# Attention with beacon keys, then two expert layers: the first sequence's queries are cut at 512, its masks become matmuls, and its last 64 queries follow between expert groups

## The chip, the cores and the metric

The kernel runs on one core of one Trainium2 chip. Its time is the device time in microseconds (us) of one execution; three runs of the kernel before gave 326.47, 326.90 and 327.72 us, with a median of 326.9 us. The core has five engines that matter here: TensorE (PE) for matmuls and transposes, ScalarE (ACT) for exponentials and activations, VectorE (DVE) for copies and sums, GpSimd (POOL) for masks and for the issue of most DMAs, and SyncE (SP) for the issue of the others. PE writes only to PSUM, a memory of few banks, from which ACT and DVE fetch the results.

## What is computed

```python
k_all = np.concatenate([beacon_k, k], axis=2)      # 8 x 8 heads, 16 + 576 keys of 64
v_all = np.concatenate([beacon_v, v], axis=2)
scores = scale * np.matmul(q, k_all.transpose(0, 1, 3, 2))
causal[:, Nb:] = np.triu(np.ones((S, S), dtype=bool), k=1)
scores = np.where(causal, -1000000000.0, scores)
a = np.exp(scores - scores.max(-1, keepdims=True))
a /= a.sum(-1, keepdims=True) + 1e-09
x = np.matmul(a, v_all)                            # then reshaped to 4608 tokens x 512
h = x @ w_in                                       # 512 x 2048
out = np.maximum(0.01 * h, h) @ w_out              # 2048 x 512
```

There are 8 sequences of 576 tokens with 8 heads of 64. Inputs and output are float32; the kernel works in bfloat16 on chip.

## The kernel before

**Pairs and steps.** Two heads make a pair (128 partitions), so there are 32 pairs, `g` = 0 to 31, four to a sequence. A pair goes through these steps, each with a letter in strings such as `"q4 v2.1 x1"` that `run` (L698) carries out one after the other. The order of the strings is the order on every engine: `tc.manual_schedule` takes it as it stands.

- `l` loads q or k of a pair (POOL issues the DMA), `V` loads a block of values, `i` and `o` load a half of the up and down weights (1 MB each in bfloat16).
- `q`, `k` (`t_q`, L231) transpose q or k in 18 small matmuls by the identity and copy the result from PSUM.
- `s` (`score`, L256) multiplies keys by queries. Keys stand on partitions in five blocks of up to 128 (`NKB`, `ROWS`, the first with the 16 beacon keys); a block is multiplied only by the queries that may see it. The four steps s0 to s3 of a pair have 512, 464, 416 and 288 columns for each head (`SCORES`, L50), the two heads in the two halves of the array. ACT takes the exponential of each step in one instruction (L276). Two score buffers of PSUM alternate (`ps_sc`, `bufs=2`).
- `m` (`mask`, L282) sets what lies under the diagonal to zero, five selections on POOL for a pair (L289).
- `v` (`value`, L374) multiplies the exponentials by the values, in two halves of 128-query tiles: t = 0, 1, 2 and t = 3, 4. A 65th column of ones gives the sum by which DVE then divides (L388, L389). `e` and `W`, `value_ahead` and `unused_ahead`, stand for beginning a half early and for fillers in its bank.
- `x` (`x_transposes`, L400) turns the result and copies it to `xT`, the experts' input.
- `w` (`unused`, L653) are fillers: matmuls of a blank tile whose result nobody reads; `w2.384` is two of 384 columns.
- `u` (`up`, L629) is one step of the first expert layer: for a chunk of 512 tokens, 128 of the 2048 hidden columns, four matmuls of 512 columns (L442) and one activation on ACT (L450). `d` (`down`) is one step of the second layer; for chunk 0 it is a quarter of the hidden dimension for 128 tokens, four matmuls (L512).

Chunk 0 is tokens 0 to 511 of sequence 0, so its first `u` needs all four pairs of that sequence.

**Opening and main loop.** The strings at L751 to L770 write out sequences 0 and 1 by hand (pairs 0 to 7) with all 16 up steps of chunk 0 and the first six down steps. The first up step comes after the `x` of pair 3, and the scores of pair 4 already stand ahead of it. Then a loop over pairs 8 to 31 sorts events by planned times and calls `fill` (L602) between them, which interleaves up and down steps. There the q and k come by DMA transposes and the scores in stretches of 512 columns (L314).

**Queues.** POOL issues the DMAs of q, k, v and weights in program order between its masks, each one waiting for the eighth before it to land. SP issues the first keys, the DMA transposes and the stores. `gT` (L429) holds an expert chunk's activations, two buffers of 16 x 512 columns for the chunks in turn.

Of the kernel before, what the change touches and what calls it, by code (L numbers as in the profile page):

```python
# [15 lines left out]
def kernel(  # L16
# [40 lines left out]
    PADS = (1392, 1728)  # L57
    BASE = [0, 512, 976, 1440, 1648]
    QT = [(0, 112), (112, 128), (240, 128), (368, 128), (496, 80)]
    NA, NK = 4, 8  # L60
# [7 lines left out]
    def acol(g, c, q0):  # L68
        if g >= LAID:
            return FLAT[c] + q0 - OFF[c]  # L70
        if c == 0:
            return 1312 if q0 == 496 else q0
        if c == 4:
            return 1648
        return BASE[c] + q0 - OFF[c]
# [13 lines left out]
    blank = singles.tile([128, 128], BF16, name="blank")  # L89
    w_in_sb = [singles.tile([128, NJ, DF // 2], BF16, name=f"w_in_sb{i}") for i in range(2)]  # L90
# [26 lines left out]
    def make_pads():  # L117
        nc.vector.memset(k_all[:, :, NB + S :], 0.0)
        for t in a_bufs:
            for c in PADS:  # L120
                nc.vector.memset(t[:, :, c : c + 48], 0.0)

    def make_ones():
        for t in v_bufs:
            nc.vector.memset(t[:, :, :, D : D + 1], 1.0)
# [3 lines left out]
    def load_w_in(i):  # L129
        n = DF // 2  # L130
        loaded["w_in", i] = nc.gpsimd.dma_start(
            out=w_in_sb[i], in_=w_in_r[:, :, i * n : (i + 1) * n]
        )
# [71 lines left out]
    def load_v_cast(b, c):  # L205
        dst = v_bufs[b % 2]
        lo = 0
        if c == 0:
            nc.gpsimd.dma_start(
                out=dst[0:NB, 0, :, 0:D], in_=beacon_v[b].rearrange("h p d -> p h d")  # L210
            )
            lo = NB
        n = ROWS[c] - lo
        nc.gpsimd.dma_start(  # L214
            out=dst[lo : ROWS[c], c, :, 0:D],
            in_=v[b, :, OFF[c] : OFF[c] + n].rearrange("h p d -> p h d"),
        )
# [13 lines left out]
    def t_q(g, which, copy):  # L231
        b, hp, grp, rows = where(g)
        dst = operand(g, which)
        ps = ps_one.tile([128, 1024], BF16, name="tp", tag="one")
        psv = ps[:, 0:S].rearrange("c (i p) -> c i p", i=RI)
        for i in range(RI):
            if (g, which) == (0, 1):
                nc.tensor.transpose(
                    psv[:, i], k_nat0[:, i].rearrange("p h d -> p (h d)"), ident[0:RP, 0:RP]
                )  # L240
                continue
            for par in range(2):
                nc.tensor.transpose(
                    psv[par * 64 : par * 64 + 64, i], qk_raw[b, grp][which][rows, par, i], ident[rows, rows]
                )
        cut = 13 if (g, which) == (0, 1) else RP
        for lo, hi, eng in ((0, cut, copy), (cut, RP, nc.vector.tensor_copy)):
            if lo < hi:
                eng(
                    out=dst.rearrange("c (p i) -> c p i", i=RI)[:, lo:hi],  # L250
                    in_=psv.rearrange("c i p -> c p i")[:, lo:hi],
                )

    probs = {}

    def score(g, n):  # L256
# [4 lines left out]
        parts = SCORES[n]  # L261
        sc = ps_sc.tile([128, 2, 512], FP32, name="sc", tag="sc")
        c0 = parts[0][3]
        for c, q0, w, col in parts:
            for par in range(2):
                ps_ = slice(par * 64, par * 64 + 64)
                nc.tensor.matmul(  # L267
                    out=sc[:, par, col - c0 : col - c0 + w],
                    lhsT=kT[ps_, c * 128 : (c + 1) * 128],
                    rhs=qT[ps_, q0 : q0 + w],  # L270
                    start=True,
                    stop=True,
                    skip_group_check=True,
                )
        w = sum(p[2] for p in parts)
        nc.scalar.activation(  # L276
            out=aT[:, :, c0 : c0 + w], in_=sc[:, :, 0:w], func=AF.Exp, scale=0.125
        )
# [66 lines left out]
    xs, avs = {}, {}  # L345

    begun = set()

    def value_matmuls(g, half, avv, ts):
# [3 lines left out]
        for t in ts:  # L353
            q0, _ = QT[t]
            for par in range(2):
                n = t % 3 * 2 + par
                for c in range(t + 1):
                    a0 = acol(g, c, q0)
                    nc.tensor.matmul(  # L359
                        out=avv[:, n, 0 : D + 1],  # L360
                        lhsT=aT[0 : ROWS[c], par, a0 : a0 + 128],
                        rhs=va[0 : ROWS[c], c, 2 * hp + par, :],
# [5 lines left out]
    def value_ahead(g):  # L368
        if (g, 0) not in avs:
            avs[g, 0] = ps_one.tile([128, 512], FP32, name="av", tag="one")  # L370
        value_matmuls(g, 0, avs[g, 0][:, 0:396].rearrange("p (n w) -> p n w", w=66), (0, 1))
        begun.add(g)

    def value(g, half):  # L374
        if half == 0:
            xs[g] = (
                headpool.tile([128, 5, 2, D], BF16, name="x_nat", bufs=4),
                headpool.tile([128, 10], FP32, name="rec"),
            )
        x_nat, rec = xs[g]  # L380
        t0, t1 = ((0, 3), (3, 5))[half]
        av = avs.pop((g, half), None)
        if av is None:
            av = ps_one.tile([128, 512], FP32, name="av", tag="one")
        avv = av[:, 0 : (t1 - t0) * 132].rearrange("p (n w) -> p n w", w=66)
        value_matmuls(g, half, avv, range(t0 + (2 if half == 0 and g in begun else 0), t1))
# [6 lines left out]
            op=ALU.mult,  # L393
        )
# [5 lines left out]
    def x_transposes(g, copy):  # L400
        b, hp = divmod(g, NPAIR)
        x_nat, _ = xs.pop(g)
        ps = ps_one.tile([128, 1024], BF16, name="tp", tag="one")
        for t, (q0, rows) in enumerate(QT):
            nc.tensor.transpose(
# [4 lines left out]
        copy(out=xT[:, hp, x_at(b) : x_at(b) + S], in_=ps[:, 0:S])  # L410
# [17 lines left out]

    gT = {}  # L429
# [235 lines left out]
    def unused_ahead(g, half, n):  # L665
        if (g, half) not in avs:
            avs[g, half] = ps_one.tile([128, 512], FP32, name="av", tag="one")
        for i in range(n):
            nc.tensor.matmul(
                out=avs[g, half][:, 400:512], lhsT=blank, rhs=blank[:, 0:112], start=True, stop=True  # L670
            )

# [19 lines left out]
    def run(steps):  # L692
        for step in steps.split():
# [7 lines left out]
            elif op == "e":  # L701
                value_ahead(*a)
# [22 lines left out]
            elif op == "W":  # L725
                unused_ahead(*a)
            elif op == "i":
                load_w_in(a[0])
# [17 lines left out]
    with order:  # L746
# [5 lines left out]
        make_identity(nc, ident, nomemset=True)  # L752
        make_ones()
        run("l1.1 l2.0 l2.1 V0.0 V0.1 l3.0 l3.1 V0.2 V0.3 V0.4 l4.0 l4.1 i0")
# [7 lines left out]
        run("q0.1 k0 w2.384 s0.0 m0.0 w3.256 s0.1 q1 s0.2 m0.1 k1 s0.3 m0.2")  # L762
        run("w2.384 s1.0 m1.0 q2 s1.1 k2 w2.384 s1.2 m1.1 w2.384 s1.3 m1.2 W0.0.4 s2.0 m2.0 W0.0.4 s2.1 W0.0.6 q3 l5.0 l5.1 s2.2 k3 w4.384 v0.0 m2.1 s2.3 i1 m2.2 W0.1.4 s3.0 m3.0 v1.0 s3.1 v0.1 s3.2 v1.1 m3.1 l6.0 l6.1 s3.3 x0.1 m3.2")
        run("v2.0 V1.0 V1.1 q4 v2.1 x1 k4.1 v3.0 v3.1 x2.1 s4.0 s4.1 x3 m4.0 V1.2 V1.3 V1.4 l7.0 l7.1 u u s4.2 s4.3 q5 k5 m4.1 m4.2 u o0 u")
        load_beacon_k(2, B, nc.gpsimd)
        run("s5.0 s5.1 m5.0 u u u s5.2 s5.3 q6 k6 m5.1 m5.2 o1 u u s6.0 s6.1 m6.0 u v4.0 u v4.1 y4 N8.0 N8.1 u s6.2 s6.3 q7 k7 m6.1 m6.2 u")
        cast_beacon_k(2, B, nc.gpsimd.tensor_copy)
        run("u v5.0 u v5.1 N9.0 s7.0 s7.1 m7.0 d x5 v6.0 v6.1 T8 d s7.2 s7.3")
        beacon_transposes(2, B)
        run("m7.1 m7.2 N9.1 u b8.2 b9.2 b10.2 b11.2 x6 v7.0 T9 v7.1 d d d N10.0 N10.1 d V2.0 V2.1 x7 t0 T10")  # L770
# [97 lines left out]
```

## Time and profile before

| what | value |
|---|---|
| median of three timed runs | 326.9 us |
| the profiled execution's own time | 325.23 us |
| its span in the profile | 323.5 us |
| PE busy, 3429 matmuls | 317.3 us (98%) |
| ACT busy | 199.3 us (62%) |
| POOL busy | 184.7 us (57%) |
| DVE busy | 146.1 us (45%) |
| first score matmul starts | 7.04 us |
| first up matmul starts | 25.25 us |
| granted PE clock | full throughout |

The profile is of one execution; times in it count from the start of the span, and the 1.7 us between the span and the execution's own time lie outside it. A row of a timeline gives start, length from the first start to the last end, engine, line, operation, what is written and read, the rows and columns of the array, the number of columns, and how many instructions follow one another. Matmuls overlap: a single one is in flight for about 0.2 us or more while the next starts, so the distance from one row's start to the next row's start says what a row takes, not its length. A waits row gives who waited for whom, the sum in us and how often.

### The profile page before, as it was taken

How to read it: one execution, taken by the hardware profiler on the slowest of the kernel's cores; microseconds unless marked ns; L12 is line 12 of the kernel's file. 1: busy time of each engine (PE TensorE's matmuls, PEld its weight loads, DVE VectorE, ACT ScalarE, POOL GpSimd, SP SyncE). 2: the span in 40 equal slices, each digit the busy share in tenths (PEclk: the TensorE clock that was granted, in tenths of full speed). 3: DMA queues.
4: the chain of work that ended last, by engine and by line, in shares of the span. 5: the costliest groups of instructions: out<-in, count | busy, mean ns of one | idle time of the engine just before them, and what ended most of it. 6: DMA issues, size and time to landing. Idle time of an engine off the chain costs nothing.

```text
span 323.5 us, 8521 instructions
## 1 busy us (share of the span) xinstructions
PE 317.3 (98%) x3429; PEld 213.4 (66%) x3429; DVE 146.1 (45%) x297; ACT 199.3 (62%) x336; POOL 184.7 (57%) x354
## 2 busy tenths in 40 slices
PE   8999999999999999999999999999999999999995
PEld 5574565445687558845888888656865785466684
DVE  3473354518446145434552455345444542325444
ACT  4969862487765786478647873786468415653420
POOL 8895968999997687659875977664221000000000
PEclk9999999999999999999999999999999999999999
DMA  8999999999999999999999999999112112000203
GB/s 140 137 206 175 147 214 120 188 165 190 157 138 169 218 147 107 124 174 80 154 192 160 110 127 115 196 128 135 52 53 79 24 54 97 2 1 32 79 20 132
DMA packets 155928, 39.93 MB, mean 123 GB/s; under 512 B 143040, under 2 KB 153152, under 8 KB 155888
## 3 DMA queue, kind: packets, MB, share of 16 engines
q0 software_dynamic: 99824, 18.54, 91.3%
q1 hardware_dynamic: 55792, 20.77, 37.1%
q8 instruction: 27, 0.44, 0.6%
q14 instruction: 13, 0.11, 0.1%
q10 hardware_dynamic: 272, 0.07, 0.1%
HBM read 37.22 MB, written 9.44 MB: 144 GB/s over the span
## 4 chain that ended last, share of the span: by engine, by line
PE 77%; DMA 10%; POOL 5%; ACT 3%; DVE 2%; issue 2%; DVEq 0%; POOLq 0%; ACTq 0%
PE acc L442 31%; PE acc L537 30%; PE av L359 6%; PE sc L314 6%; DMA w_out_sb<-in_moe_w_out_dram 4%; PE acc L512 4%; DMA w_in_sb<-in_moe_w_in_dram 4%; POOL aT L289 2%; DMA gsum<-in_k_dram 2%; ACT aT L333 2%; POOL gsum L158 2%; ACT aT L329 1%; DVE p L565 0%; ACT gT L450 0%; DVE u L565 0%
## 5 line engine op out<-in xcount | busy, mean ns | idle before, releaser
L442 PE MATMUL acc<-xT,w_in_sb 128*128 128x512 bf16 (+1 forms) x640 | 135.7, 358 | 0.3 <-ACT aT L329 0.3
L450 ACT ACTIVATE gT<-acc 128x512 bf16<-128x512 f32 x144 | 82.8, 621 | 46.4 <-PE acc L442 46.2
L442 PEld LDWEIGHTS <-w_in_sb 128*128 128x128 bf16 x640 | 59.6, 98 | 52.4 <-issue 2.9
L289 POOL TENSOR_SCALAR_AFFINE_SELECT aT<-aT 128x256 bf16<-128x256 bf16 (+2 forms) x160 | 59.7, 404 | 51.7 <-ACT aT L329 30.9
L537 PEld LDWEIGHTS <-gT 128*128 128x128 bf16 x512 | 48.8, 98 | 9.1 <-issue 1.8
L333 ACT ACTIVATE aT<-sc 128x1024 bf16<-128x1024 f32 (+3 forms) x64 | 51.8, 895 | 0.0
L537 PE MATMUL acc<-w_out_sb,gT 128*128 128x256 bf16 x384 | 46.2, 273 | 0.4 <-ACT gT L450 0.4
L329 ACT ACTIVATE aT<-sc 128x512 bf16<-128x512 f32 (+3 forms) x64 | 29.0, 522 | 27.9 <-PE sc L314 27.7
L388 DVE RECIPROCAL rec<-av 128x6 f32<-128x6 f32 (+1 forms) x64 | 12.0, 188 | 67.0 <-PE av L359 66.3
L359 PEld LDWEIGHTS <-aT 128*128 128x128 bf16 (+1 forms) x960 | 36.7, 98 | 8.3 <-issue 0.6
L537 PEld LDWEIGHTS <-gsum 128*128 128x128 bf16 x384 | 36.5, 98 | 6.2 <-issue 0.4
L359 PE MATMUL av<-v_aug,aT 128*128 128x65 bf16 (+1 forms) x960 | 39.4, 194 | 0.3 <-ACT gT L450 0.2
L214 POOL DMA_DIRECT2D v_aug<-in_v_dram x40 | 34.2, 859 | 4.1 <-DMA w_in_sb<-in_moe_w_in_dram 3.4
L568 ACT COPY p<-acc 128x512 f32<-128x512 f32 (+1 forms) x25 | 14.5, 580 | 35.6 <-PE acc L537 35.6
L171 POOL DMA_DIRECT2D k_nat<-in_k_dram x48 | 34.9, 733 | 1.3 <-DMA w_out_sb<-in_moe_w_out_dram 0.6
L171 POOL DMA_DIRECT2D q_nat<-in_q_dram x48 | 34.8, 731 | 0.6 <-issue 0.3
L389 DVE TENSOR_TENSOR x_nat<-av,rec 128x384 bf16<-128x384 f32 (+1 forms) x64 | 31.4, 491 | 2.2
L537 PE MATMUL acc<-w_sum,gsum 128*128 128x256 bf16 x256 | 31.9, 273 | 0.0
L276 ACT ACTIVATE aT<-sc 128x1024 bf16<-128x1024 f32 (+3 forms) x32 | 25.9, 875 | 3.5 <-PE sc L267 3.5
L620 DVE TENSOR_TENSOR gsum<-gT 128x1024 bf16<-128x1024 bf16 x16 | 11.0, 688 | 28.1 <-ACT gT L450 28.1
L314 PE MATMUL sc<-qT,kT 64*128 64x80 bf16 (+22 forms) x384 | 22.0, 250 | 0.3
L314 PEld LDWEIGHTS <-kT 64*128 64x128 bf16 x384 | 12.9, 94 | 10.9 <-issue 7.6
(62 smaller groups left out, 227.3 us busy)
## 6 DMA issues: line engine op xcount, KB each, us to landing
out_dram<-p SPq DMA_DIRECT2D x26, 256.0 KB, 3.2
q_nat<-in_q_dram POOLq DMA_DIRECT2D x48, 72.0 KB, 5.5
k_nat<-in_k_dram POOLq DMA_DIRECT2D x48, 72.0 KB, 5.0
v_aug<-in_v_dram POOLq DMA_DIRECT2D x24, 128.0 KB, 6.1
w_in_sb<-in_moe_w_in_dram POOLq DMA_DIRECT2D x2, 1024.0 KB, 11.7
w_out_sb<-in_moe_w_out_dram POOLq DMA_DIRECT2D x2, 1024.0 KB, 11.7
out_dram<-u SPq DMA_DIRECT2D x8, 256.0 KB, 2.7
gsum<-in_q_dram POOLq DMA_DIRECT2D x8, 144.0 KB, 6.9
```

The costliest lines, as they stand in the source:

```text
L171: nc.gpsimd.dma_start(out=t[:, :, par], in_=(q, k)[which][b, 2 * hp + par].rearrange("(t p) d -> p t d", p=NR),)
L214: nc.gpsimd.dma_start(out=dst[lo : ROWS[c], c, :, 0:D], in_=v[b, :, OFF[c] : OFF[c] + n].rearrange("h p d -> p h d"),)
L276: nc.scalar.activation(out=aT[:, :, c0 : c0 + w], in_=sc[:, :, 0:w], func=AF.Exp, scale=0.125)
L289: nc.gpsimd.affine_select(out=view, in_=view, compare_op=ALU.is_ge, fill=0.0, base=128 - n if lo == 0 else 0, channel_multiplier=-1, patte ...
L314: nc.tensor.matmul(out=(sc[par] if apart else sc[:, par])[:, at : at + b - a], lhsT=kT[ps_, c * 128 : (c + 1) * 128], rhs=qT[ps_, q0 : q0 ...
L329: nc.scalar.activation(out=probs[g][:, par, lo:hi], in_=sc[par][:, at : at + hi - lo], func=AF.Exp, scale=0.125)
L333: nc.scalar.activation(out=probs[g][:, :, lo:hi], in_=sc[:, :, at : at + hi - lo], func=AF.Exp, scale=0.125)
L359: nc.tensor.matmul(out=avv[:, n, 0 : D + 1], lhsT=aT[0 : ROWS[c], par, a0 : a0 + 128], rhs=va[0 : ROWS[c], c, 2 * hp + par, :], start=(c = ...
L389: nc.vector.tensor_tensor(out=x_nat[:, t0:t1].rearrange("p t e d -> p (t e) d"), in0=avv[:, :, 0:D], in1=rec[:, n0:n1, None].to_broadcast( ...
L442: nc.tensor.matmul(out=acc[:, lo:hi], lhsT=w_in_cols(fc, j), rhs=xT[:, j, x0 : x0 + hi - lo], start=(j == 0), stop=(j == NJ - 1), skip_gro ...
L450: nc.scalar.activation(out=gT[i][:, fc, :], in_=acc, func=AF.Prelu, alpha=0.01)
L537: nc.tensor.matmul(out=acc[:, lo : lo + HD], lhsT=left(i, n, fc, tile), rhs=right(n, fc), start=(lo == 0 and fc == 0), stop=(fc == HF - 1) ...
```

## The change

Sequence 0 only (`g < NPAIR`):

- Its scores cover queries 0 to 511 (`CUT`), in three steps of 512, 400 and 432 columns (`EARLY`) for four. The masks of these blocks are added to the scores in PSUM by matmuls of the identity by a `bias` tile (`hide`), ten for a pair, and the POOL masks of sequence 0 go. The bias is made on POOL between the identity and the next DMA issue.
- The value halves become t = 0, 1 and t = 2, 3, 4; the last tile and key block have 16 rows.
- The other 64 queries are copied aside by DVE when q is transposed (`rest_q`, in the still unused `gT` of chunk 1). Their scores, in 64 columns for each key block, follow as steps `L0` to `L3` between up steps of chunk 0 (`rest_scores`); their values for two pairs each as `Y0` and `Y1`, and their transposes as `Z0` and `Z1`, after the sixteenth up step.
- Steps `q4`, `k4`, `s4.0` and `s4.1` stand after the first up steps, no longer ahead of them; values and `x` of pairs 4 to 7 come after all up steps of chunk 0. Eleven down steps for six stand ahead of the main loop.
- Loads: q and k of pair 3 ahead of all values; the last block of values in two parts; the first half of the up weights in two parts, ahead of pairs 4 and 5; the second half ahead of pairs 6 and 7.
- Fillers from the first scores to the first up: 27 of 384 columns, where there were 10 of 384, 3 of 256 and 18 of 112.

```diff
-    PADS = (1392, 1728)
+    PADS = ((1344, 112), (1728, 48))
+    CUT = 512
+    REST = S - CUT
+    EARLY = [[(0, 0, 512, 0)], [(1, 112, 400, 512)], [(2, 240, 272, 912), (3, 368, 144, 1184), (4, 496, 16, 1328)]]
...
+    def make_bias():
+        nc.gpsimd.affine_select(
+            out=bias, in_=blank, compare_op=ALU.is_ge, fill=-32768.0,
+            base=0, channel_multiplier=-1, pattern=[[1, 128]],
+        )
...
+        if which == 0 and g < NPAIR:
+            nc.vector.tensor_copy(out=rest_q[:, g], in_=dst[:, CUT:S])
...
+        if g < NPAIR:
+            for c, q0, w, col in parts:
+                w, at = min(w, 112 if c == 0 else 128), 16 if c == 0 else 0
+                for par in range(2):
+                    hide(sc[:, par, col - c0 : col - c0 + w], at)
...
+    def hide(out, at):
+        nc.tensor.matmul(out=out, lhsT=ident, rhs=bias[:, at : at + out.shape[1]], start=False, stop=True)
+
+    def rest_scores(g):
+        kT = qk[g][1]
+        sc = ps_sc.tile([128, 2, 512], FP32, name="sc", tag="sc")
+        for c in range(NKB):
+            for par in range(2):
+                ps_ = slice(par * 64, par * 64 + 64)
+                nc.tensor.matmul(
+                    out=sc[:, par, c * REST : (c + 1) * REST],
+                    lhsT=kT[ps_, c * 128 : (c + 1) * 128],
+                    rhs=rest_q[ps_, g],
...
+        for par in range(2):
+            hide(sc[:, par, 4 * REST : 5 * REST], CUT - OFF[4])
+        nc.scalar.activation(out=rest_a[:, g], in_=sc[:, :, 0 : NKB * REST], func=AF.Exp, scale=0.125)
...
+                    rows = min(ROWS[c], CUT - OFF[c]) if g < NPAIR else ROWS[c]
...
+    def rest_values(p):
...
+        for e in range(2):
+            for par in range(2):
+                for c in range(NKB):
+                    nc.tensor.matmul(
+                        out=avv[:, 2 * e + par, 0 : D + 1],
+                        lhsT=rest_a[0 : ROWS[c], 2 * p + e, par, c * REST : (c + 1) * REST],
+                        rhs=v_bufs[0][0 : ROWS[c], c, 2 * (2 * p + e) + par, :],
...
+            rows = min(rows, end - q0)
...
-        run("l1.1 l2.0 l2.1 V0.0 V0.1 l3.0 l3.1 V0.2 V0.3 V0.4 l4.0 l4.1 i0")
+        run("l1.1 l2.0 l2.1 l3.0 l3.1 V0.0 V0.1 V0.2 V0.3 V0.4.0.16 i0.0.2 i0.1.2 l4.0 l4.1 l5.0 l5.1 V0.4.16 i1 l6.0 l6.1 V1.0 V1.1")
...
-        run("q0.1 k0 w2.384 s0.0 m0.0 w3.256 s0.1 q1 s0.2 m0.1 k1 s0.3 m0.2")
-        run("w2.384 s1.0 m1.0 q2 s1.1 k2 w2.384 s1.2 m1.1 w2.384 s1.3 m1.2 W0.0.4 s2.0 m2.0 W0.0.4 s2.1 W0.0.6 q3 l5.0 l5.1 s2.2 k3 w4.384 v0.0 m2.1 s2.3 i1 m2.2 W0.1.4 s3.0 m3.0 v1.0 s3.1 v0.1 s3.2 v1.1 m3.1 l6.0 l6.1 s3.3 x0.1 m3.2")
-        run("v2.0 V1.0 V1.1 q4 v2.1 x1 k4.1 v3.0 v3.1 x2.1 s4.0 s4.1 x3 m4.0 V1.2 V1.3 V1.4 l7.0 l7.1 u u s4.2 s4.3 q5 k5 m4.1 m4.2 u o0 u")
+        run("q0.1 k0 w2.384 s0.0 w1.384 s0.1 q1 s0.2 w2.384 k1 w2.384 s1.0 q2 w1.384 s1.1 w1.384 k2 s1.2 w1.384 q3 w1.384 s2.0 k3 s2.1 w3.384 s2.2 w2.384 s3.0 v0.0 w1.384 s3.1 v1.0 w1.384 s3.2 v2.0 w2.384 v3.0 w7.384")
+        run("v0.1 v1.1 v2.1 x0.1 v3.1 x1.1 w1.384 x2.1 w1.384 x3.1 u u L0 q4 u k4.1 u s4.0 s4.1 m4.0 V1.2 V1.3 V1.4 u L1 u s4.2 s4.3 m4.1 m4.2 l7.0 l7.1 o0 q5 k5 u u")
         load_beacon_k(2, B, nc.gpsimd)
-        run("s5.0 s5.1 m5.0 u u u s5.2 s5.3 q6 k6 m5.1 m5.2 o1 u u s6.0 s6.1 m6.0 u v4.0 u v4.1 y4 N8.0 N8.1 u s6.2 s6.3 q7 k7 m6.1 m6.2 u")
+        run("s5.0 s5.1 m5.0 u u L2 u s5.2 s5.3 m5.1 m5.2 o1 q6 k6 u u s6.0 s6.1 m6.0 u L3 u s6.2 s6.3 m6.1 m6.2 u Y0 N8.0 N8.1 q7 k7 Z0 Y1")
         cast_beacon_k(2, B, nc.gpsimd.tensor_copy)
-        run("u v5.0 u v5.1 N9.0 s7.0 s7.1 m7.0 d x5 v6.0 v6.1 T8 d s7.2 s7.3")
+        run("v4.0 s7.0 s7.1 m7.0 v4.1 y4 Z1 v5.0 s7.2 s7.3 v5.1 N9.0 d v6.0 x5 d v6.1 T8 d")
         beacon_transposes(2, B)
-        run("m7.1 m7.2 N9.1 u b8.2 b9.2 b10.2 b11.2 x6 v7.0 T9 v7.1 d d d N10.0 N10.1 d V2.0 V2.1 x7 t0 T10")
+        run("m7.1 m7.2 N9.1 d b8.2 b9.2 b10.2 b11.2 x6 v7.0 T9 v7.1 d d d N10.0 N10.1 d V2.0 V2.1 x7 t0 T10 d d d")
```

## The prediction

> **What bounds the kernel now.** I read the page's busy shares and chain of waits first, then the busy times by stretch, then TensorE's (PE's) timeline.
>
> ```profile
> PE 317.3 (98%) x3429; PEld 213.4 (66%) x3429; DVE 146.1 (45%) x297; ACT 199.3 (62%) x336; POOL 184.7 (57%) x354
> PE 77%; DMA 10%; POOL 5%; ACT 3%; DVE 2%; issue 2%; DVEq 0%; POOLq 0%; ACTq 0%
> 7.04:25.25 18.21, 17.98 (x369) 11.93 (x368) 11.15 (x25) 14.64 (x20) 17.06 (x37) 1.00 1.75 174
> 25.25:52.24 26.99, 26.60 (x371) 14.59 (x369) 11.16 (x27) 21.19 (x32) 19.21 (x37) 1.00 2.04 168
> ```
>
> PE is the chain. The last two lines are my two stages (columns: length, then busy PE, PE loads, DVE, ACT, POOL): from the first scores (7.04) to the first up matmul (25.25), and from there to the third quarter of the first down tile (52.24). PE is busy in both, but busy is not peak, so I price PE by the distance between starts in its timeline:
>
> ```profile
> 15.33 0.47 PE L243 MATMUL tp<-ident,gsum 64*64 64x64 bf16 x18
> 15.73 0.82 PE L657 MATMUL av<-blank 128*128 128x384 bf16 x4
> 16.39 0.53 PE L359 MATMUL av<-v_aug,aT 128*128 128x65 bf16 x12
> ...
> 27.54 0.76 PE L243 MATMUL tp<-ident,gsum 64*64 64x64 bf16 x36
> 28.23 1.90 PE L442 MATMUL acc<-xT,w_in_sb 128*128 128x512 bf16 x8
> 30.06 0.59 PE L267 MATMUL sc<-qT,kT 64*128 64x512 bf16 x4
> ...
> 37.97 1.03 PE L442 MATMUL acc<-xT,w_in_sb 128*128 128x512 bf16 x4
> 38.83 0.72 PE L359 MATMUL av<-v_aug,aT 128*128 128x65 bf16 x18
> 39.39 1.03 PE L442 MATMUL acc<-xT,w_in_sb 128*128 128x512 bf16 x4
> 40.35 0.48 PE L267 MATMUL sc<-qT,kT 64*128 64x336 bf16 x8
> ```
>
> Four 384-column fillers take 16.39-15.73 = 0.66, so 0.16 us each (2.4 columns per ns). 18 value matmuls take 0.56 (about 30 ns each), 36 transposes 0.69 (19 ns). Four up matmuls take 0.86 ahead of value matmuls (37.97 to 38.83) but 0.96 ahead of scores (39.39 to 40.35): a change of the array's shape (128*128 to 64*128) costs 0.10. Eight ahead of scores take 1.83 = 8 x 0.216 + 0.10. I take 0.097 per change.
>
> Does this price list close? By the instruction order, the first stage of before has 13.1 us of columns (score pairs, which run side by side in two halves, 3.2; q and k transposes 2.7; values 3.5; x transposes 1.0; fillers 2.8) and 41 changes of shape x 0.097 = 4.0: 17.1 against 18.2 elapsed, so 1.1 of real waits. The second stage: 24.4 + 18 x 0.097 = 26.15 against 26.65 up to 51.9. So PE's own work sets both stages. ACT, with 14.64 of 18.21 and 21.19 of 26.99, is not the bound.
>
> **What the Trainium skill says.** "TensorEngine Tiling (Array Packing)", Tiling Modes (Key Properties): "Changing tiling mode (not just tile) drains the TensorE". The trace agrees: 0.10 us per change above. Same page, Performance Considerations (Instruction Overhead): about 60 cycles per matmul however narrow; here 65 columns take 29 to 31 ns, which I use as floor. "TensorE: Matmul & The Clock Gate", Part 3 (The mechanism): matmuls keep strict order, so a filler is paid in full whether needed or not; the trace shows all of them in program order.
>
> **The change, part by part.**
>
> *First stage (s0 to the first up).* Scores of a pair shrink from 1680 to 1344 columns: 4 x 336 / 2.4 = -0.56. Transposes and scores of pair 4 (q4, k4, s4.0, s4.1) move behind the first up: -0.69 - 0.41. Values and x transposes stay in number (120 and 20). The 40 mask matmuls are new: per pair 2 x (112+3x128+16) columns, in all 1.7, with the floor for the narrow ones 1.9. Fillers go from 10 of 384, 3 of 256 and 18 of 112 columns (2.76) to 27 of 384: 4.32, +1.56. Changes of shape go from 41 to 56, +1.45: a score group is now followed by 128-row masks, and the twelve 16-row products and transposes (L424 and L503 of the changed kernel, from cutting at query 512) are built as 32*128 tiles, two changes each, partly shared. Sum: 20.35 against 17.1, +3.2. Waits I leave nearly alone (-0.2): twenty POOL masks vanish (0.5 us of PE load waits on them in the whole opening), but the copy of q0's last 64 columns stands on DVE ahead of the first key copy (unseen; between 0.1 and 0.35, I take 0.28 with its wait on ACT), and everything is behind it. First up: about 25.25 + 3.0 = 28.3.
>
> *What could hide that?* ACT's exponentials of this stage fall from 16 (spaced 0.92, 0.82, 0.74, 0.64) to 12, about 9.7 us for 12.6. ACT had not been the limit, so this buys nothing while PE has 20 us to do. DMA neither: the POOL queue delivers in order; values of sequence 0 were down at 18.8, and the first half-megabyte of up weights, now right behind them, should be down near 21 (half of the 4.3 us that the full half took to arrive), long before 28. The mask constant on POOL (0.32, as the identity) delays the second keys' issue by as much; they are wanted at 10 us. The extra DMA from each split costs POOL 0.7 to 0.8 us of issue, hidden as the first up comes late.
>
> *Second stage and after.* The late scores L0..L3: 40 narrow matmuls in pairs 0.5, 8 masks 0.25. Late values Y0, Y1: 40 x 29 ns = 1.15; transposes 0.1. q4, k4, s4.0, s4.1 arrive: +1.1. Changes of shape: +22 = 2.1 (u to L, L to its masks, u to q4, Y in 64 columns). Sum +5.2 (the model of all matmuls gives 5.1). None of it lies under another engine's work: PE is full to the end, so what is added is paid.
>
> *Waits there.* A late score takes one of the two score buffers between s4.1 and s4.2, so s4.3 waits until ACT has done s4.0, s4.1, an up's activation, L1's exponential: by ACT's spacing 0.92+0.82+0.5+0.7 against PE's u, L1, u, s4.2 of about 2.5. From 0.2 to 0.75 per pair, three times: 1.0 (0.4 to 2.2). In return some waits of before go (columns: us in all, times, longest):
>
> ```profile
> PE acc L512 <- DMA w_out_sb<-in_moe_w_out_dram: 0.3, 1, 0.3
> PE acc L442 <- ACT aT L329: 0.3, 1, 0.3
> ```
>
> The second down weights landed at 52.2 and PE now comes for them later; first stretch of scores the same (its keys landed at 59.6). With what surrounds them 0.5 to 1.4; I take 1.0. More downs ahead of the main loop (11 for 6) only change order. SP's queue keeps its order, with later starts.
>
> *Sum*: 3.2 + 5.1 - 0.2 + 1.0 - 1.0 = +8.1; I use +8. The profiled execution took 325.23 (span 323.5 and 1.7 around it), which gives 333.2; it lies 1.7 below the median of 326.9, which gives 334.9.
>
> **Rivals.**
>
> *Small tiles come cheap.* No row of before shows a 32*128 tile. If changing to it drains nothing, 24 changes fall away: -2.3, so +5.6, 332.5. Lower bound, with masks also streaming behind the scores at no change: +4. Against: 64*128, 64*64 and 128*64 all cost 0.10.
>
> *Buffers bite.* The score-buffer waits come out at 0.75 each (+1.2), and the first stage's own waits (s1.0 on k1's copy 0.45, values at the 37 ns they had before 20 us instead of 30: 0.7) add 1.2: +10.5, 337.4.
>
> *ACT sets the first up* (not slower). In before the first up follows the last exponential's end by 25.25-21.09 = 4.2:
>
> ```profile
> 17.20 3.89 ACT L276 ACTIVATE aT<-sc 128x576 bf16<-128x576 f32 x5 [0.84 <-PE sc L267]
> 24.98 0.43 PE L405 MATMUL tp<-ident,x_nat 112*128 112x112 bf16 x5
> 25.25 1.95 PE L442 MATMUL acc<-xT,w_in_sb 128*128 128x512 bf16 x8
> ```
>
> If the exponentials were the limit and PE only filled time, they would end near 7.9+9.7 = 17.6 and the first up come at 21.8: -3.5. With +5.1 behind it and up to 1.6 of waits gone, 0.0: 326.9, and faster if the first up comes before about 21.7. For: the stage is full of fillers. Against: even without fillers PE has 16 us from 7.3.
>
> That the change does not do what it says is ruled out by the order: all its steps stand where it puts them.
>
> **How the numbers follow.** Main case 0.55, small tiles cheap 0.22, buffers bite 0.10, ACT sets it 0.13. The last splits at no change: faster by over 0.5% 0.07, within 0.5% 0.06, the others all slower: 0.87. Half a per cent (1.6 us) is about what a measurement of this kernel can tell from no change. The range reaches from inside the cheap-tile case, with its waits gone, 329.5, to just past buffers bite, 337.5; it leaves out the last rival and a little above.
>
> **What would show it.** First up at 28.3 (27 to 29) for 25.25; mask matmuls 47 to 55 ns apart and 0.10 lost at each switch, also around the 16-row ones; PE gaps at s4.3, s5.3, s6.3 with ACT's late exponential as releaser; no wait for down weights; the stretch from first up to third down 4 us longer. A first up before 25 would make me wrong, as would a second stage no longer than before.

## The result, and the profile after

The changed kernel took 337.8 us (median of six) against 326.4 for the kernel before (median of six in the same rounds): a ratio of 1.034, with a 95% interval of 1.031 to 1.038. It is slower, as forecast, by 11 us where 8 were forecast, and lies 0.3 us above the top of the range. In some executions, the first profiled one of the changed kernel among them, PE's clock ran at half through part of the opening: the ratio leaves these out (337.6 us without them), the profile shown here is of a further execution (336.72 us, span 334.9), and of other profiles with such an opening I read only what comes behind it, unless the text says otherwise.

The page of the changed kernel, with its busy shares and its chain of waits:

```profile
PE 327.2 (98%) x3549; PEld 219.0 (65%) x3549; DVE 146.0 (44%) x305; ACT 200.2 (60%) x338; POOL 179.5 (54%) x337
...
PE 81%; ACT 8%; DMA 3%; DVE 3%; issue 2%; SPq 2%; DVEq 0%; ACTq 0%; POOLq 0%
```

PE is busy 9.9 us longer and still 98%; in the chain ACT has gone from 3% to 8%, and DMA from 10% to 3%. The busy times by stretch (length, then PE, PE loads, DVE, ACT, POOL, clock, DMA share, GB/s), first scores to first up, first up to the third quarter of the first down tile ("the third down"), and from there to the end; the last line is that end of the kernel before:

```profile
7.44:28.92 21.48, 21.00 (x356) 13.87 (x356) 11.04 (x26) 12.32 (x15) 12.11 (x18) 1.00 1.61 186
28.92:61.01 32.09, 30.93 (x452) 16.57 (x452) 9.94 (x24) 24.59 (x39) 19.16 (x37) 1.00 1.13 125
61.01:334.90 273.89, 269.41 (x2690) 184.62 (x2686) 121.99 (x237) 160.36 (x281) 142.00 (x269) 1.00 1.13 113
52.24:323.50 271.26, 266.88 (x2637) 182.83 (x2636) 121.20 (x229) 160.60 (x281) 142.56 (x269) 1.00 1.20 115
```

So the stages are 3.27 and 5.10 us longer than before, the first scores start 0.40 later (7.44 for 7.04), and what follows the third down is 2.63 longer (273.89 for 271.26). Sum: 11.4, the difference of the two spans.

What part of that is PE's own work? The prediction's price list (columns at 2.4 per ns, 0.097 for a change of shape), run over every matmul of both orders, gives 17.1 and 20.35 for the first stage, 26.15 and 29.33 for the second, 259.7 and 261.6 for the rest: +3.25, +3.18 and +1.94, in all 8.4. The forecast had 3.2 + 5.1 = 8.3. (This 8.4 is worked out from the order, not measured.) What is left over of the measured stretches, the waits, is +0.4 ahead of the first stage, nothing in it, +1.9 in the second and +0.7 behind: 3.0 us. The forecast had -0.2 there.

These are two traces, and waits differ from one execution to the next. The opening of the kernel before stands unchanged in the experiment with three more down steps below; its trace has 19.12 us in the first stage (0.65 of it a wait for a POOL mask) and 28.16 in the second (0.84 of it a wait for down weights), and without its fillers the kernel before took 272.3 behind the third down. So a single wait term is known to about 1 us only. The changed kernel's second stage is steadier: 32.1 or 32.2 in every trace that has the same steps there.

Much of the 3 us can be read line by line. PE's waits in the changed kernel (us in all, times, longest), which answer to the two lines for the weights and for `acc` shown of before:

```profile
PE sc L295 <- DVE kT L269: 0.7, 2, 0.4
PE sc L295 <- ACT gT L339: 0.6, 2, 0.3
PE sc L377 <- DVE x_nat L446: 0.4, 1, 0.4
```

The waits for down weights and for the first stretch's bank are gone, as forecast. In their place stand waits for the copy of the keys, for the late exponential (`gT L339` is ACT's instruction for an `L` step), and new ones in the main loop. The first kind begins with the first keys: DVE copies away q's last 64 columns ahead of them, so their copy starts at 7.10 (first two lines), for 6.69 in the kernel before (third line):

```profile
6.88 0.18 DVE L274 COPY gT<-qT 128x64 bf16<-128x64 bf16 x1 [0.71 <-ACT qT L269]
7.10 0.82 DVE L269 COPY kT<-tp 128x117 bf16<-128x117 bf16 x2
6.69 0.82 DVE L249 COPY kT<-tp 128x117 bf16<-128x117 bf16 x2 [0.60 <-PE tp L238]
```

The timeline shows where the second kind sits:

```profile
35.66 0.32 PE L329 MATMUL sc<-gT,kT 64*128 64x64 bf16 x10
35.91 0.23 PE L314 MATMUL sc<-bias,ident 128*128 128x64 bf16 x2
35.98 1.03 PE L538 MATMUL acc<-xT,w_in_sb 128*128 128x512 bf16 x4
36.94 0.35 PE L295 MATMUL sc<-qT,kT 64*128 64x336 bf16 x4
37.58 0.30 PE L295 MATMUL sc<-qT,kT 64*128 64x208 bf16 x4 [0.29 <-ACT gT L339]
37.81 0.75 PE L263 MATMUL tp<-ident,gsum 64*64 64x64 bf16 x36
```

The two score steps from 36.94 to 37.81 take 0.87 where they need 0.41 (43.09 to 43.50 in an experiment below): s4.3 stands 0.46 for its buffer. The same happens at s5.3 (0.26) and s6.3 (0.45), and s7.3 stands 0.39 for an ordinary exponential; L1 and L3 lose 0.18 each beyond their change of shape.

### The profile page after: what moved, and what is told of

The parts are those of the page before. It is cut to its first block, busy times and chain, and to the rows that moved or that the text cites. A ratio compares the mean times of both kernels' runs of the same rounds, so it can differ in the third digit from the quotient of the medians.

```text
span 342.2 us, 8723 instructions
## 1 busy us (share of the span) xinstructions
PE 331.5 (97%) x3521; PEld 220.9 (65%) x3549; DVE 146.0 (43%) x305; ACT 200.4 (59%) x338; POOL 179.5 (52%) x337
## 4 chain that ended last, share of the span: by engine, by line
PE 84%; ACT 7%; DMA 3%; issue 2%; DVE 2%; SPq 0%; DVEq 0%; ACTq 0%; POOLq 0%
PE acc L538 31%; PE acc L633 27%; PE av L424 8%; PE sc L377 5%; PE acc L608 4%; PE sc L295 3%; ACT aT L396 2%; PE tp L263 2%; DMA xT<-x_nat 2%; PE av L753 2%; ACT gT L546 2%; DMA gsum<-in_q_dram 1%; PE sc L314 1%; ACT aT L309 1%; ACT aT L392 1%
## 5 line engine op out<-in xcount | busy, mean ns | idle before, releaser
L538 PE MATMUL acc<-xT,w_in_sb 128*128 128x512 bf16 (+1 forms) x615 | 133.7, 357 | 1.7 <-issue 0.5
L352 POOL TENSOR_SCALAR_AFFINE_SELECT aT<-aT 128x256 bf16<-128x256 bf16 (+2 forms) x140 | 52.6, 401 | 76.1 <-ACT aT L392 31.8
L396 ACT ACTIVATE aT<-sc 128x1024 bf16<-128x1024 f32 (+3 forms) x64 | 51.9, 899 | 0.0
L424 PE MATMUL av<-v_aug,aT 128*128 128x65 bf16 (+1 forms) x960 | 40.5, 194 | 0.6 <-DMA v_aug<-in_v_dram 0.6
L309 ACT ACTIVATE aT<-sc 128x1024 bf16<-128x1024 f32 (+5 forms) x28 | 24.0, 907 | 12.4 <-PE sc L314 9.9
```

What stands on the lines that cost most here:

```text
L309: nc.scalar.activation(out=aT[:, :, c0 : c0 + w], in_=sc[:, :, 0:w], func=AF.Exp, scale=0.125)
L352: nc.gpsimd.affine_select(out=view, in_=view, compare_op=ALU.is_ge, fill=0.0, base=128 - n if lo == 0 else 0, channel_multiplier=-1, patte ...
L396: nc.scalar.activation(out=probs[g][:, :, lo:hi], in_=sc[:, :, at : at + hi - lo], func=AF.Exp, scale=0.125)
L424: nc.tensor.matmul(out=avv[:, n, 0 : D + 1], lhsT=aT[0:rows, par, a0 : a0 + 128], rhs=va[0:rows, c, 2 * hp + par, :], start=(c == 0), stop ...
L538: nc.tensor.matmul(out=acc[:, lo:hi], lhsT=w_in_cols(fc, j), rhs=xT[:, j, x0 : x0 + hi - lo], start=(j == 0), stop=(j == NJ - 1), skip_gro ...
```

## The experiments

Each run was compared with the kernel before in the same rounds; the time is the median, to be held against 337.6 for the changed kernel (six executions, 336.7 to 338.0). Ratios are to the kernel before; those of the experiments on the changed kernel overlap in part, so gains of 1 to 2 us also need what the traces show.

### The changed kernel again

> The changed kernel once more, for a profile at full clock. Theory (PE's own work is paid in full): its timed runs at full clock had spans of about 335.9 us and 306.5 us lay behind the first up in the first profile, so the first up should stand near 29.4 us, 4.2 us later than in the kernel before, and PE's waits from there to the end about 3 us above those of before. Rival (a slow clock early on is part of the change's cost): the clock is below full in the first 25 us here too, and the first up is near 35.7.

336.72 and 337.59 us; ratio 1.029 (1.019 to 1.040). First up at 28.92: in the forecast's span of 27 to 29, at its upper end, and some 0.5 earlier than this experiment expected.

### Fillers: all 27 out, 20 out, and those of the kernel before out

```diff
-        run("q0.1 k0 w2.384 s0.0 w1.384 s0.1 q1 s0.2 w2.384 k1 w2.384 s1.0 q2 w1.384 s1.1 w1.384 k2 s1.2 w1.384 q3 ... w7.384")
+        run("q0.1 k0 w2.384 s0.0 s0.1 q1 s0.2 k1 s1.0 q2 s1.1 k2 s1.2 q3 ...")
+        run("q0.1 k0 w2.384 s0.0 w1.384 s0.1 q1 s0.2 w2.384 k1 w2.384 s1.0 q2 w1.384 s1.1 w1.384 k2 s1.2 q3 ...")
```

> The changed kernel without the 27 fillers of 384 columns between the first scores and the first up. Theory (PE's own work sets the first stage of the changed kernel, so each filler is paid): 27 x 0.16 = 4.3 us and a few changes of shape fewer, so 4 to 5 us less, about 333. Rival (ACT's exponentials, the loads of values or the up weights set the first up, and fillers stand where PE would wait): less than 1 us gained, about 337.

338.5 us (335.7 to 338.8; ratio 1.031, 1.024 to 1.039): nothing gained. The busy times of that kernel by stretch:

```profile
4.87:8.28 3.41, 2.22 (x41) 1.30 (x38) 1.95 (x5) 0.64 (x1) 3.41 (x6) 1.00 1.11 159
8.28:21.93 13.65, 12.79 (x180) 7.89 (x178) 5.94 (x12) 8.68 (x10) 8.98 (x14) 0.50 1.92 180
21.93:25.34 3.41, 3.41 (x79) 2.94 (x78) 2.81 (x9) 2.12 (x3) 2.32 (x4) 1.00 1.28 204
```

PE runs at half clock for 13.65 us here, and the first up came at 29.70. So this run doesn't price the fillers. Nor does it show that they hold the clock up: PE was busy for only 2.22 us of the 3.41 ahead of that stretch, but the fillers that are gone would stand behind it, and the changed kernel with all of them did the same in its first profile (2.28 of 3.41 us busy, then 17.07 at half clock).

In the kernel before, all fillers behind the first scores go in the same way.

> The kernel before without its fillers between the first scores and the first up (2.76 us of columns). Theory (PE sets the first stage there too, as the prediction had it): about 2.8 us less, 323.6. Rival (ACT's chain of 16 exponentials, back to back from 7.5 to 16.4 us, sets the first stage of before and the fillers only stand in for waits): no change, 326.4, within 0.5 us; the first up stays near 25.2.

327.7 us (20 executions; ratio 1.002, 0.999 to 1.005). No difference that can be measured. In the profiled execution the first up came at 27.27 for 25.25, not earlier: again at half pace (18 transposes in 0.63 us for 0.40). So this says nothing on whether ACT set the stage in the kernel before. (What ran back to back from 7.5 to 16.4 there were eleven exponentials; the sixteenth ends at 21.09.)

> The 20 fillers that stand between s1.2 and the first up are left out; those before s1.2 stay, so that PE's clock has risen as it did. At 0.16 us they are 3.2 us of PE. Theory P (PE's own work sets the first up, as in the prediction): first up some 3 us earlier than 28.9, at 25.5 to 26.5. Rival A (the exponentials on ACT set it, fillers only fill): the first up stays within 0.7 us of 28.9, and PE's idle time appears ahead of values and score steps with ACT as releaser. Rival C: the clock falls to half again, and the first up comes at 29 or later.

334.9 us (five executions, 334.4 to 335.4; the profiled one took 339.2, and the ratio, 1.025, 1.021 to 1.029, includes it): 2.7 less for 20 fillers of 0.16 each, 3.2. So most of a filler is paid, against rival A. Its first up at full pace is not on record; the last experiment, without the same fillers, has one.

### Mask matmuls out

```diff
-        if g < NPAIR:
-            for c, q0, w, col in parts:
...
-                    hide(sc[:, par, col - c0 : col - c0 + w], at)
```

> The changed kernel without the 40 mask matmuls of sequence 0, which is left unmasked for its first 512 queries. Theory (paid in full): 1.9 us of columns and the changes of shape around them, about 12 x 0.1: 3 us less, 334.5. Rival (masks hide behind waits of PE for ACT or loads): under 0.5 us.

336.25 us in the profiled execution; two others took 340.3 and 340.8, and the ratio on record (1.035, 1.025 to 1.046) is of all three. In the profile the first up came at 26.86, 2.06 earlier where 3 were expected, and the second stage was the same (32.10); yet the end came only 0.4 earlier than in the changed kernel's profile. This is where the rest went, in PE's timeline of this kernel:

```profile
107.54 1.04 PE L628 MATMUL acc<-w_sum,gsum 128*128 128x256 bf16 x8
108.41 0.53 PE L419 MATMUL av<-v_aug,aT 128*128 128x65 bf16 x12
110.78 0.35 PE L419 MATMUL av<-v_aug,aT 80*128 80x65 bf16 x6 [1.83 <-DMA v_aug<-in_v_dram]
110.96 1.04 PE L628 MATMUL acc<-w_sum,gsum 128*128 128x256 bf16 x8
```

The last 80 rows of sequence 3's values landed at 110.73; PE waited 2.0 us for them. POOL issued them at 103.20, and the transfer took 7.53. With masks, the same rows went out at 105.27 and landed in 5.32, at 110.59, just as PE came:

```profile
105.27 0.73 POOL L234 DMA_DIRECT2D v_aug<-in_v_dram  x1
```

```profile
110.48 0.72 PE L424 MATMUL av<-v_aug,aT 128*128 128x65 bf16 x18
```

So this issue moves with PE's progress, about 5.3 us ahead of the use, and the transfers take 5.3 to 7.5. In the kernel before there were 8.2 us (issued 91.23, used from 99.43 on), for 6.5 of transfer.

### Loads ahead of pair 4's masks

My first theory was that the loads as a whole run late: POOL stands for 10.8 us at the first mask of pair 4, which waits for ACT's exponential of s4.0, now behind the first up; value loads and the down weights are queued behind it.

```profile
35.68 0.37 POOL L352 TENSOR_SCALAR_AFFINE_SELECT aT<-aT 128x224 bf16<-128x224 bf16 x1 [10.82 <-ACT aT L309]
36.00 1.77 POOL L234 DMA_DIRECT2D v_aug<-in_v_dram  x2
```

```diff
-        run("... u u L0 q4 u k4.1 u s4.0 s4.1 m4.0 V1.2 V1.3 V1.4 u L1 u s4.2 s4.3 m4.1 m4.2 l7.0 l7.1 o0 q5 k5 u u")
+        run("... u u V1.2 V1.3 V1.4 l7.0 l7.1 o0 L0 q4 u k4.1 u s4.0 s4.1 m4.0 u L1 u s4.2 s4.3 m4.1 m4.2 q5 k5 u u")
```

> The three blocks of values of sequence 1, the q and k of pair 7 and the first half of the down weights are issued by POOL ahead of the masks of pair 4, where the changed kernel issues them behind. Theory L (loads are a second bound): POOL's queue now has no gap at 33 to 40 us, sequence 3's values land 3 to 6 us ahead of 105, but at full clock PE was only just not waiting for them, so the time falls by 0 to 1 us (336 to 337.5). Rival P (PE's own work only): the same time, and a gap that stays or moves elsewhere. Only together with the next run does this tell the two apart.

336.7 us (336.3 to 337.8; ratio 1.032, 1.027 to 1.036). A difference of 0.9 that the spread doesn't separate from none, and the gap had only moved: POOL now issued all that and then stood 8.6 us at the same mask.

> As the run before, and the 40 mask matmuls of sequence 0 are left out too, so its exponentials stay unmasked. Without the earlier loads this cut brought the first up forward by 2.06 us, and PE lost 2.0 us again at 110.8 in a wait for sequence 3's values. Theory L: with the loads earlier that wait is gone and the 2 us reach the end: 334 to 335.3 against 336.3 to 337.6 for the run before. Rival (the DMA engines themselves are the bound, so that issuing earlier lands nothing earlier): the wait stays, within 0.5 us of the run before.

335.9 us (335.2 to 336.7; ratio 1.029, 1.023 to 1.034): 0.8 below the run above, not 2, with a wait of 1.1 us for the same values, issued 6.6 us before they landed. Theory L falls: earlier loads in the opening do not help a load whose issue stands in the main loop at a fixed distance ahead of its use.

### Down steps left to the main loop

What shortened that distance? The changed kernel does eleven down steps ahead of the main loop and the kernel before six; the main loop spreads what is left over its first stretches. PE's timeline of the changed kernel there:

```profile
79.24 2.97 PE L538 MATMUL acc<-xT,w_in_sb 128*128 128x512 bf16 x13
82.14 1.17 PE L377 MATMUL sc<-qT,kT 64*128 64x176 bf16 x14
83.25 3.63 PE L538 MATMUL acc<-xT,w_in_sb 128*128 128x512 bf16 x16
86.89 1.21 PE L424 MATMUL av<-v_aug,aT 128*128 128x65 bf16 x30
87.94 1.03 PE L538 MATMUL acc<-xT,w_in_sb 128*128 128x512 bf16 x4
88.90 0.21 PE L377 MATMUL sc<-qT,kT 64*128 64x96 bf16 x1
89.54 0.83 PE L377 MATMUL sc<-qT,kT 64*128 64x96 bf16 x15 [0.43 <-DVE x_nat L446]
```

Only up steps, four in a row, each with an activation on ACT, and score stretches that wait: those from 82.14, 88.90, 94.79 and 100.35 take 0.35, 0.64, 0.29 and 0.20 more than the 0.76 of a stretch that doesn't.

```diff
-        run("... V2.0 V2.1 x7 t0 T10 d d d")
+        run("... V2.0 V2.1 x7 t0 T10")
```

> The three down steps at the end of the last opening string are taken out there; the main loop does them itself, between its score stretches and values. Theory W (the down steps done ahead were the work that covered the main loop's first waits): of the 1.2 us that PE waits at score stretches between 82 and 101 us about half goes, and the last value block of sequence 3 has some 2.5 us more between its issue and PE's coming for it (there were 5.3 us, exactly its landing time). 336.4 to 337.3 for 337.6. Rival (they only change order, as the prediction said): 337.6 within 0.3, with the same waits at other places.

336.2 us (335.6 to 337.5; ratio 1.032, 1.029 to 1.036), 1.4 less; the times alone hardly part it from the changed kernel. In its timeline up and down steps alternate ahead of the stretch from 82.70, which has no wait:

```profile
79.15 1.03 PE L538 MATMUL acc<-xT,w_in_sb 128*128 128x512 bf16 x4
80.01 1.03 PE L608 MATMUL acc<-w_out_sb,gT 128*128 128x512 bf16 x4
80.87 1.03 PE L538 MATMUL acc<-xT,w_in_sb 128*128 128x512 bf16 x4
81.74 1.03 PE L608 MATMUL acc<-w_out_sb,gT 128*128 128x512 bf16 x4
82.70 0.83 PE L377 MATMUL sc<-qT,kT 64*128 64x176 bf16 x14
```

The next two stretches, from 88.82 and 95.00, don't wait either; two waits of 0.4 stand at other places (77.4 and 99.1). What follows the third down is 272.9 long:

```profile
62.77:335.70 272.93, 267.24 (x2668) 184.07 (x2686) 122.27 (x237) 160.48 (x281) 141.88 (x269) 1.00 1.16 114
```

It is 272.9 in each of the three profiles without these down steps (this one, the next and the last below), and 273.6 to 274.7 in eight that keep them (the changed kernel's two and the six experiments on its opening that leave its masks and late work in). So the three steps cost about 1.3 us there. In five of the eight, the changed kernel's first profile among them, PE waited 0.3 to 1.0 us of it for sequence 3's last values; in the three without, it never did. Those values are now issued 8.3 us ahead of their group of products (103.21 to 111.53) for 5.2 (105.27 to 110.48).

> As the changed kernel without its three last down steps of the opening, and the 40 mask matmuls of sequence 0 are left out too (its exponentials stay unmasked). Theory W: with 8.4 us for 5.3 us between issue and use of sequence 3's last values, the wait of 2.0 us (1.1 with the earlier loads) is gone, and the 2.06 us that the first stage saves reach the end: 334.1 within 0.4, for 336.1 with masks. Rival (loads are late whatever their place): the wait is back, 335.3 or more.

333.4 and 334.1 us (ratio 1.022, 1.018 to 1.025): 2.4 below the run above. The wait for values is gone (issued 8.3 us ahead, landed in 7.4), and what the first stage saves reaches the end:

```profile
112.18 1.04 PE L628 MATMUL acc<-w_sum,gsum 128*128 128x256 bf16 x8
113.06 0.72 PE L419 MATMUL av<-v_aug,aT 128*128 128x65 bf16 x18
113.62 1.04 PE L628 MATMUL acc<-w_sum,gsum 128*128 128x256 bf16 x8
```

> On the kernel before, three more down steps at the end of the opening strings (nine ahead of the main loop for six), and nothing else. In the changed kernel taking three away there saved 1.5 us. Theory W (down steps done ahead are missing as cover in the first stretch of the main loop): 0.5 to 1.5 us slower than 326.4, with new waits of PE at score stretches between 70 and 95 us, and 2.5 us less between the issue of sequence 3's last value block and its use (8.2 us before, landing in 6.5). Rival (order only, as the prediction said): 326.4 within 0.3.

327.0 us (ratio 1.000, 0.998 to 1.003): no difference that can be measured, against theory W as I had put it. Nine down steps ahead cost nothing in the kernel before; there 7.1 us stayed between issue and use of the same values (95.02, group at 102.09), for a transfer of 6.4. So the price is not one for each down step moved. One part is the wait for values, which comes when the distance falls under the transfer's time (2.0 us without masks). Why the score stretches of the changed kernel wait more, and those of the kernel before with nine down steps ahead don't cost it time, stays open; that no down step is left between the ups is read from two timelines, not tried by itself.

### Late scores elsewhere

L1 directly behind its group (second line) or apart from it (third line), L2 and L3 likewise, with L3 behind Y0 in the third:

```diff
-        run("... u L1 u s4.2 s4.3 m4.1 m4.2 l7.0 l7.1 o0 q5 k5 u u")
+        run("... u u s4.2 s4.3 L1 m4.1 m4.2 l7.0 l7.1 o0 q5 k5 u u")
+        run("... u u s4.2 s4.3 m4.1 m4.2 l7.0 l7.1 o0 q5 k5 u L1 u")
```

> The late scores L1, L2 and L3 stand behind s4.3, s5.3 and s6.3, no longer between the two pairs of score steps. Theory (the waits of 0.45, 0.26 and 0.45 us at s4.3, s5.3 and s6.3 are for the score buffer that the late score took): they go, some 1.1 us less from first up to third down (32.1 to about 31), if nothing comes in their place. Rival: ACT is as late as PE in this stage, so the wait moves to the late score itself or to the next pair's first scores, and the stage stays at 32 within 0.3.

341.6 us (339.5 to 341.8; ratio 1.044, 1.040 to 1.049): 4 us slower, of which 2.4 lie between first up and third down in its profile (34.49 for 32.09); the rest isn't explained. The waits moved to the late scores and grew (1.41, 1.04 and 1.41 us idle):

```profile
42.64 0.48 PE L295 MATMUL sc<-qT,kT 64*128 64x336 bf16 x8
44.53 0.32 PE L329 MATMUL sc<-gT,kT 64*128 64x64 bf16 x10 [1.41 <-ACT aT L309]
44.78 0.23 PE L314 MATMUL sc<-bias,ident 128*128 128x64 bf16 x2
```

Behind s4.3 both buffers are full, and ACT is still at the exponentials of the group.

> L1 and L2 stand one up step after q5, k5 and q6, k6, and L3 behind Y0, so that no late score lies between or directly behind the score steps of a pair. Behind s4.3 directly they had cost 3 us more, with waits of 1.57, 1.20 and 1.57 us for ACT. Theory B (two score buffers, with an ACT that is just as late as PE in each group of score steps): now ACT has caught up when the late score comes; the waits at s4.3, s5.3, s6.3 (1.16 us together) and at L1 and L3 (0.36) go and nothing replaces them: first up to third down 30.6 for 32.1, in all 336.1. Rival A (ACT's work of the stage is the bound as a whole, not its bunching): the waits come back at the next scores, 32 within 0.3, 337.6.

336.0 us (335.5 to 336.5; ratio 1.031, 1.027 to 1.034): 1.6 less. First up to third down took 30.4 for 32.1, and neither the score steps nor the late score wait:

```profile
43.09 0.48 PE L295 MATMUL sc<-qT,kT 64*128 64x336 bf16 x8
43.50 0.75 PE L263 MATMUL tp<-ident,gsum 64*64 64x64 bf16 x36
44.19 1.04 PE L538 MATMUL acc<-xT,w_in_sb 128*128 128x512 bf16 x3
45.16 0.32 PE L329 MATMUL sc<-gT,kT 64*128 64x64 bf16 x10
```

So it is bunching on two buffers (theory B), not ACT's work as a whole.

### The late work left out, and the 16-row tiles

L0 to L3, Y0, Y1, Z0 and Z1 go; one of the strings, and what fills their place:

```diff
-        run("... u Y0 N8.0 N8.1 q7 k7 Z0 Y1")
+        run("... u N8.0 N8.1 q7 k7")
+        nc.vector.memset(xT[:, :, CUT:S], 0.0)
```

> The late work is left out: no scores, exponentials, values and transposes for sequence 0's last 64 queries (L, Y, Z); their 64 columns of the experts' input are zeroed in one DVE instruction. By the prediction's own list this takes away 0.5 + 0.25 + 1.15 + 0.1 of columns and some 14 changes of the array's shape at 0.097, so 3.4 us; theory (waits were what the prediction lacked): the 1.5 us of waits at and behind L go with it, 332.2 to 333.2 for 337.6. Rival (only its columns cost, the waits stay): 334.2 within 0.4.

333.1 us (332.7 to 333.1; ratio 1.021, 1.018 to 1.025): 4.5 less, in the expected span. The stage is 27.9 long for 32.1, in spite of a wait of 0.9 us for pair 7's keys at 50.7; behind it 1.0 is lost in one for sequence 3's values (at 107.6).

```diff
-                    rows = min(ROWS[c], CUT - OFF[c]) if g < NPAIR else ROWS[c]
+                    rows = ROWS[c]
-        run("... V0.3 V0.4.0.16 i0.0.2 i0.1.2 l4.0 l4.1 l5.0 l5.1 V0.4.16 i1 ...")
+        run("... V0.3 V0.4 i0.0.2 i0.1.2 l4.0 l4.1 l5.0 l5.1 i1 ...")
```

> The last key block of sequence 0 is loaded whole ahead of the up weights, and its value products use all 80 rows (the masked ones are zero) in place of 16, so these are built as 128*128 tiles like their neighbours and no longer as 32*128. By the prediction's price of 0.097 us for each of 16 changes of shape the first up comes 1.5 us earlier (27.4 for 28.9), the time is 336.0 to 336.4. Rival (the prediction's own: small tiles cost nothing): no difference, 337.6 within 0.3.

335.5 us (335.0 to 335.9; ratio 1.029, 1.025 to 1.032): 2.1 less. The same 72 value products, first in the changed kernel, then in this one:

```profile
22.26 3.51 PE L424 MATMUL av<-v_aug,aT 128*128 128x65 bf16 x72
25.70 0.50 PE L503 MATMUL tp<-ident,x_nat 112*128 112x112 bf16 x5
```

```profile
28.54 2.38 PE L424 MATMUL av<-v_aug,aT 128*128 128x65 bf16 x72
30.76 0.49 PE L503 MATMUL tp<-ident,x_nat 112*128 112x112 bf16 x5
```

3.44 against 2.22 us from start to start, and 1.15 against 0.76 for the other 24: 1.61 for 16 changes of shape, 0.10 each. The rival that small tiles are free is out. (What the time gained beyond 1.6, some 0.5 us, I can't place; it is within the spread of the executions.)

### Four edits together

80 rows, no fillers from s1.2 on, late scores apart, three down steps left to the main loop.

> Four of the edits together on the changed kernel: 80 rows in place of 16 (2.1 us alone), no fillers from s1.2 on (2.7), late scores apart from score groups (1.55), three down steps left to the main loop (1.5). If the four are separate terms they add up to 7.85: 329.7 (329.2 to 330.4), still some 3 us above the kernel before, since the late work of 4.5 us stays. Rival (savings of the first stage are lost again, at the exponentials or in a later wait for loads): 331.5 or more.

330.4 us (four executions within 0.05; a fifth took 335.1, and the ratio, 1.014, 1.009 to 1.019, includes it): 7.2 less for a sum of the single gains of 7.8. In its profile, at full pace, the first up came at 25.37 for 28.92, after a first stage of 17.40 for 21.48: 4.1 of the 4.8 us of fillers and shape changes taken out. So PE's own work sets the first up of the changed kernel. About what the sum lacks is lost there, where score steps now wait for exponentials three times:

```profile
17.02 0.37 PE L295 MATMUL sc<-qT,kT 64*128 64x272 bf16 x6 [0.22 <-ACT aT L309]
...
18.73 0.35 PE L295 MATMUL sc<-qT,kT 64*128 64x400 bf16 x2 [0.20 <-ACT aT L309]
...
19.65 0.36 PE L295 MATMUL sc<-qT,kT 64*128 64x272 bf16 x6 [0.17 <-ACT aT L309]
```

It is still nearly 4 us slower than the kernel before (326.7 in the same rounds). No version tried beats that one.

## Why the prediction was right in its direction and wrong in its size

*PE is the bound, and added PE work is paid.* Right in the main. The same list, run over the new order, gives +8.4 for +8.3; that repeats the forecast's arithmetic. What tests it are the first stage, measured at 3.27 longer for 3.25, and the runs without masks (-2.1 to -2.4 for 3), 16-row tiles (-2.1 for 1.6), 20 fillers (-2.7 for 3.2) and the late work (-4.5 for 3.4 and its waits): the size is right to within 1 us each. (For the masks the 3 counted twelve changes of shape; the orders with and without masks differ by about three in that stage, so that an estimate by the list is 2.2.)

*Small tiles, 0.097 each, with a rival at nothing.* Right at 0.10; the 22% for the rival was caution that no row of before supported, and it put the low end at 329.5.

*First stage: "Waits I leave nearly alone (-0.2)".* The stage's own waits stayed as they were, and the first scores came 0.40 later: the first key copy stands behind the copy of q's columns on DVE, priced at 0.28 and then set off against waits for POOL masks. Those were waits of two weight loads of this stage (0.23 us each, at 17.71 and 23.60 in before), and without them the stage's waits came out no smaller. 0.6 too little; first up at 28.92 for 28.3.

*Score-buffer waits: 1.0 (0.4 to 2.2).* The mechanism was right and the three waits measured 1.17. The term was 0.9 too small, as the same crowding also cost 0.39 at s7.3 and 0.18 each at L1 and L3: the stage's waits rose by 1.9. Moving the late scores apart took 1.7 out of the stage.

*Relief: "With what surrounds them 0.5 to 1.4; I take 1.0".* This is the step that failed, 1.7 of the 3.3 us by which the sum was short. The waits named did go, but the 1.0 did not come off the total: behind the third down waits rose by 0.7. The main part of it that the runs show is *"More downs ahead of the main loop (11 for 6) only change order"*: with three of the eleven given back, this stretch lost about 1.3 us of waits and was 272.9 long, where before's 271.3 and the 1.9 of listed work make 273.2. So some relief came, and the down steps done early used it up. They would have been work for PE where score stretches wait for ACT and DVE. I had asked of each edit where its own wait goes, and not of this one what the steps had covered where they stood. It is no general rule: in the kernel before, three more down steps ahead changed nothing that can be measured, and why stays open.

*"DMA neither".* Right for the first up. It missed that a load in the main loop had only 5.2 us left ahead of its use; in the trace shown that just sufficed, in the changed kernel's first profile PE waited 0.6 us, and it ate savings of two other edits.

*Rivals.* "Buffers bite" named 337.4 and the time was 337.8, but by a different sum: its second-stage waits came (1.9 for 2.2), its 1.0 of first-stage waits came only as 0.4, and the relief that it kept did not come. "ACT sets the first up" is out for the changed kernel: without masks its first up came at 26.86, and with 20 fillers and the small tiles gone at 25.37, for 28.92. That 337.4 came so near is luck.

## What to carry to other kernels

Price the waits as carefully as the work: here a list of columns and shape changes gave the work about rightly, and nearly all of the error was in waits set down as small and of both signs. When steps are moved ahead, ask what they covered in their old place, and how many us are left there between each load's issue and its use. And beware of an extra user of a double buffer inside or directly behind the group that fills both halves: here it cost 1.7 us inside, 2.4 more directly behind, and moved away from the group it didn't wait.

## What the runs showed of the hardware

A change of the array's shape took 0.10 us also into and out of the 16-row tiles: 16 changes among 96 products of 65 columns, 1.61 us in all.

In the profile without fillers PE ran the opening at half clock for 13.65 us, four times 3.41, and in the first profile of the changed kernel for 17.07, five times; the stretch of full clock ahead was 3.41 long in both. The Trainium skill's "TensorE: Matmul & The Clock Gate", Part 1 (What's actually happening), gives a free-running window of 3413 ns on whose activity the clock is set, and these lengths agree with it. What the page doesn't lead one to expect is that a PE busy for 12.79 of those 13.65 us (16.65 of 17.07) stayed at half: being busy in the profile was not enough to get the clock back. Why, these runs don't show. The page of a profile can also miss it: that of the kernel before without fillers says full throughout, while 18 transposes took 0.63 us for 0.40; its clock record has no entry ahead of 20.67 us. The distance of equal instructions told it here.

The same 80-row load of values took 5.3 to 7.5 us from issue to landing at the same place of the order in different kernels, so a margin of 5.2 us is none here.
